# A two-layer convolution and feed-forward kernel: the inverse transform of layer–block pairs three to five by float32 products

## The chip, the cores and the metric

The kernel runs on one core of one Trainium2 chip. The engines that matter here are TensorE (PE, with its weight loads as PEld), VectorE (DVE), ScalarE (ACT), GpSimd (POOL) and SyncE (SP), which issues most DMAs. The metric is the device time of one execution in microseconds (us): 1112.5 us before, the median of three runs between 1112.49 and 1115.72 us.

## The reference, cut to what matters

Two layers, each of them a long convolution followed by a gated feed-forward block, on 2048 rows of 512 channels:

```
def _A_ref(u, ...):                      # K: a kernel of 2048 taps per channel
    Kf = rfft(pad(K)); Uf = rfft(pad(u))
    y = irfft(Uf * Kf)[:L]               # a causal convolution along the rows
    return y + u * Dskip
def _B_ref(x, w_gate, w_up, w_down):
    return (silu(x @ w_gate) * (x @ w_up)) @ w_down

x = x + _A_ref(_layernorm(x), ...)
x = x + _B_ref(_layernorm(x), ...)
x = x + _A_ref(_layernorm(x), ...)
x = x + _B_ref(_layernorm(x), ...)
```

## The kernel before

**Blocks and pairs.** The 2048 rows are cut into four blocks of 512. A pair is (layer, block), and the eight pairs run in the order of the table `SEQ`: (0,0), (0,1), (0,2), (1,0), (0,3), (1,1), (1,2), (1,3). Below they are called the first to the eighth pair. Each pair has a convolution (`ssm`, two calls of `ssm_half`, one for each half of the channels) and a feed-forward part (`ffn`, two halves of 256 rows). The first 300 us or so generate the convolution's taps and their spectra, split the feed-forward weights into two half-precision parts, and run the first pairs' convolutions; from there on the loop over pairs runs.

**The convolution.** `forward` transforms a normalised block into four spectra per half. `ssm_half` takes four steps (`s`), one for each spectrum. In each it multiplies the spectra of this block and of earlier ones with the spectra of the taps (L810) and adds them up (L813): block b takes b+1 products. Then L818 and L819 combine the real and imaginary products, and L765, L766, L831 to L843 form the four vectors `v` that are to be transformed back (`r` = 0 to 3). All of this is DVE work on float32 tiles, and a vector `v` has 2 x 256 columns. The spectra of earlier blocks and of the taps come by DMA from SP (L806 into `w`, L808 into `uu`, three buffers each).

**The inverse transform** (`inverse`, L770 to L783) multiplies each `v` with constant matrices on PE and collects two results in one PSUM tile `pi`; `result` (L785 to L791) adds that tile to the block `xt`. There are two forms. Where the pair's place in `SEQ` is below `INV`, PE multiplies the float32 `v` with the float32 constants `ei`: two products of 256 columns. Otherwise (`half`) ACT writes the upper half-precision part of the scaled `v` (L774), DVE writes the rest of it (a call of `stt` at L775, recorded under the helper's line L230, into the tile `yl`), and PE adds up six half-precision products of 256 columns:

```
terms = [(eih[:, r, i, le], yl[:, ly, i]) for i in range(2) for le, ly in ((0, 0), (0, 1), (1, 0))]
```

`result` then scales the sum back (`stt`, L230 again) where the float32 form adds it as it is (L791). The constants `ei` and `eih` lie in the same place, the first quarter of the tile `mix`; `eih` is loaded over `ei` by SP at L743, when the first pair of the half-precision form begins. So that load waits for the last float32 inverse.

**The feed-forward part.** Each half of `ffn` makes five large tiles `pgu` of 48 products of 128x256 (L930, L931, L933) and one small one in `remainder` (L897 to L899), in a PSUM pool of two buffers that `pgu` and `py` share. Each `pgu` is read out by ACT (L936) and DVE (L937), split by ACT (L938) and DVE (L939), and the last products (L945 to L947) go into `py`, which DVE adds to the block row by row (L950). PE can't begin the tile after the next one before DVE has read this one.

**What sets the order.** From the second pair on, the framework's scheduler decides the order on each engine when the kernel is built; on the chip each engine then goes through its list strictly. The convolution of pair i+1 is written ahead of the feed-forward part of pair i, and the read-outs of the feed-forward part and the inverse products have a raised priority (`BOOST`). Where its plan shows DVE free, the scheduler fills it with convolution work of later pairs, as far as buffers and data allow. The convolution of the eighth pair needs the feed-forward result of the fifth, (0,3).

Of the kernel before, what the change touches and what calls it, by code (L numbers as in the profile page):

```python
# [37 lines left out]
TB = 256  # L38
BOOST = 1 << 20
HALF = 2  # L40
INV = 2
LOW = [a for a in range(1, 33) if a % 2] + [8, 16, 24, 32]
SEQ = ((0, 0), (0, 1), (0, 2), (1, 0), (0, 3), (1, 1), (1, 2), (1, 3))

# [31 lines left out]
def kernel(ctx, tc, x, a_re, a_im, b_re, b_im, c_re, c_im, log_dt, d_skip,  # L76
# [663 lines left out]
    def ssm(layer, b):  # L740

        if (layer, b) == SEQ[INV]:
            nc.sync.dma_start(eih, c_eih)  # L743
# [3 lines left out]
    def ssm_half(layer, b, h):  # L747
        first = layer == 0 and b == 0
        half = SEQ.index((layer, b)) >= INV
        hs = slice(h * HD, (h + 1) * HD)  # L750
# [551 lines left out]
```

## Time and profile before

| | |
|---|---|
| median of three runs | 1112.5 us |
| the profiled execution: its own time / its span | 1118.76 us / 1117.0 us |
| granted TensorE clock over the span | 0.982 |
| instructions | 22795 |
| PE busy / DVE busy / ACT busy, share of the span | 93% / 87% / 49% |
| POOL busy, share of the span | 9% |
| HBM traffic over the span | 118 GB/s |
| chain that ended last: DVE / PE / issue / DMA | 43% / 32% / 11% / 7% |

The page's busy shares are means over unlike stages: DVE makes the taps at first, DVE and PE share the middle, and the last 117 us are the feed-forward part of the last pair, in which DVE has little to do. Matmuls are pipelined, so a PE row's duration (272 ns for a product of 128x256 in half precision) is longer than the distance from one start to the next; what such a product costs is read from the starts. The same holds for DVE to a smaller extent. An idle stretch of an engine is put down to the instruction that ended it.

### The profile page before, as it was taken

What the parts mean: (1) busy time and instruction counts of PE and PEld (TensorE: products, weight loads), DVE (VectorE), ACT (ScalarE), POOL (GpSimd) and SP (SyncE); (2) the same over time, 40 slices, a digit from 0 to 9 for tenths busy, and PEclk for the clock granted to TensorE, in tenths of its full rate; (3) what the DMA queues carried; (4) which work ended last, traced back from release to release, by engine and by line L of the source; (5) the groups of instructions that cost most, each with busy time, mean ns of one, the idle gap of its engine ahead of it and who ended that gap; (6) DMA issues with size and microseconds to landing.
All of it is one profiled execution on the core that took longest, in us unless ns stands there. A gap on an engine that the chain in (4) does not pass through costs nothing.

```text
span 1117.0 us, 22795 instructions
## 1 busy us (share of the span) xinstructions
PE 1034.6 (93%) x9302; PEld 812.1 (73%) x9302; DVE 969.8 (87%) x1405; ACT 548.9 (49%) x1093; POOL 105.1 (9%) x163
## 2 busy tenths in 40 slices
PE   2989999998788999899999999989999999999998
PEld 1868888887676768686858677767768686786774
DVE  8999999999999998999999989999994899972221
ACT  6989999942483245464553154524315532143210
POOL 0112222220000010110000011100000000000000
PEclk9989999998999999999999999999999999999999
DMA  5367777767765455422453562354343244302000
GB/s 207 123 174 174 170 169 178 186 182 269 234 214 96 147 158 188 152 76 54 146 141 100 144 210 86 109 167 112 132 138 109 67 138 147 123 20 56 2 25 20
DMA packets 125003, 149.23 MB, mean 134 GB/s; under 512 B 50897, under 2 KB 75985, under 8 KB 124130
## 3 DMA queue, kind: packets, MB, share of 16 engines
q1 hardware_dynamic: 112994, 122.27, 36.1%
q0 software_dynamic: 11904, 25.50, 9.8%
q8 instruction: 73, 1.20, 0.5%
q14 instruction: 32, 0.26, 0.1%
HBM read 97.66 MB, written 33.82 MB: 118 GB/s over the span
## 4 chain that ended last, share of the span: by engine, by line
DVE 43%; PE 32%; issue 11%; DMA 7%; ACT 4%; POOL 2%; SPq 1%; DVEq 0%; POOLq 0%; ACTq 0%
PE pgu L930 5%; PE pgu L933 4%; PE pgu L931 4%; PE pw L542 4%; DVE t L810 4%; DVE yk L813 3%; DVE yk L810 3%; DMA mix<-nn 3%; DVE g L483 3%; PE py L945 3%; PE py L946 2%; PE py L947 2%; DMA n<-xdr 2%; DVE sg L937 2%; DVE g L497 2%
## 5 line engine op out<-in xcount | busy, mean ns | idle before, releaser
L930 PE MATMUL pgu<-mix,wsl 128*128 128x256 f16 x1280 | 300.4, 274 | 11.9 <-DVE sg L937 5.3
L931 PE MATMUL pgu<-mix,wsl 128*128 128x256 f16 x1280 | 300.2, 274 | 0.0
L933 PE MATMUL pgu<-mix,wsl 128*128 128x256 f16 x1280 | 196.2, 274 | 0.0
L945 PE MATMUL py<-wsl,hh 128*128 128x512 f16 (+1 forms) x352 | 136.0, 386 | 17.8 <-DVE xg L950 15.0
L931 PEld LDWEIGHTS <-wsl 128*128 128x128 f16 x1280 | 125.7, 98 | 31.1 <-issue 14.3
L930 PEld LDWEIGHTS <-wsl 128*128 128x128 f16 x1280 | 125.7, 98 | 18.5 <-issue 1.2
L947 PE MATMUL py<-wsl,hl 128*128 128x512 f16 (+1 forms) x352 | 135.7, 385 | 1.9 <-DVE hl L939 1.8
L933 PEld LDWEIGHTS <-wsl 128*128 128x128 f16 x1280 | 125.8, 98 | 15.5
L946 PE MATMUL py<-wsl,hh 128*128 128x512 f16 x320 | 123.8, 387 | 0.0
L936 ACT ACTIVATE sg<-pgu,sc 128x512 f32<-128x512 f32 x80 | 54.5, 681 | 137.0 <-PE pgu L933 136.9
L813 DVE TENSOR_TENSOR yk<-yk,t 128x1024 f32<-128x1024 f32 x96 | 116.7, 1215 | 0.4
L810 DVE TENSOR_TENSOR t<-uu,w 128x1024 f32<-128x1024 f32 x96 | 116.6, 1215 | 0.1
L937 DVE SCALAR_TENSOR_TENSOR sg<-pgu,sc,sg 128x512 f32<-128x512 f32 x80 | 59.5, 744 | 54.6 <-ACT sg L936 54.5
L938 ACT ACTIVATE hh<-sg 128x512 f16<-128x512 f32 x80 | 50.2, 627 | 86.9 <-DVE sg L937 86.9
L542 PE MATMUL pw<-kt,ek 128*128 128x256 f32 (+1 forms) x384 | 90.8, 373 | 0.0
L542 PEld LDWEIGHTS pw<-kt,ek 128*128 128x128 f32 x384 | 72.3, 193 | 8.5
L946 PEld LDWEIGHTS <-hh 128*128 128x128 f16 (+1 forms) x352 | 34.9, 99 | 56.8 <-issue 21.7
L507 PE MATMUL pk<-re,g 128*32 128x64 f32 x1024 | 65.1, 317 | 2.7 <-DMA g<-g 1.6
L939 DVE TENSOR_TENSOR hl<-sg,hh 128x512 f16<-128x512 f32 x80 | 54.7, 684 | 14.4 <-ACT hh L938 14.4
L947 PEld LDWEIGHTS <-hl 128*128 128x128 f16 (+1 forms) x352 | 34.9, 99 | 43.4 <-issue 3.0
L508 PE MATMUL pk<-im,g 128*32 128x64 f32 x1024 | 63.2, 301 | 0.0
L945 PEld LDWEIGHTS <-hh 128*128 128x128 f16 (+1 forms) x352 | 34.9, 99 | 35.6 <-issue 2.9
(265 smaller groups left out, 2007.1 us busy)
## 6 DMA issues: line engine op xcount, KB each, us to landing
uu<-udr SPq DMA_DIRECT2D x96, 256.0 KB, 3.0
w<-wdr SPq DMA_DIRECT2D x96, 256.0 KB, 2.7
g<-g POOLq DMA_DIRECT2D x6, 1024.0 KB, 9.1
udr<-fu POOLq DMA_DIRECT2D x22, 256.0 KB, 2.9
udr<-u SPq DMA_DIRECT2D x16, 256.0 KB, 3.4
n<-xdr SPq DMA_DIRECT2D x4, 1024.0 KB, 7.1
kdr<-ks SPq DMA_DIRECT2D x6, 512.0 KB, 3.1
kt<-kdr SPq DMA_DIRECT2D x24, 128.0 KB, 3.0
```

The costliest lines, as they stand in the source:

```text
L507: PE.matmul(o, lhsT=g[:, 0, :, d], rhs=re[:, 0:64, d], start=True, stop=False, tile_position=(0, 32 * grp))
L508: PE.matmul(o, lhsT=g[:, 1, :, d], rhs=im[:, 0:64, d], start=False, stop=True, tile_position=(0, 32 * grp))
L542: PE.matmul(pw[:, i], lhsT=e, rhs=kt[:, :, c + 4 * k0:4 * k1:4, :].rearrange("p g k d -> p k g d"), start=c == 0, stop=c == 3)
L810: V.tensor_tensor(t, uu.unsqueeze(2).to_broadcast([P, NQ, 2, 2, DC]), w.unsqueeze(3).to_broadcast([P, NQ, 2, 2, DC]), OP.mult)
L813: V.tensor_tensor(yk, yk, t, OP.add)
L930: PE.matmul(o, lhsT=wgu(wi, k, 0)[:, fs], rhs=nh[:, k], start=k == 0, stop=False)
L931: PE.matmul(o, lhsT=wgu(wi, k, 1)[:, fs], rhs=nh[:, k], start=False, stop=False)
L933: PE.matmul(o, lhsT=wgu(wi, k, 0)[:, fs], rhs=nlo[:, k], start=False, stop=k == 3)
L937: V.scalar_tensor_tensor(sg, pgu[:, 1], sc6[:, 4:5], sg, OP.mult, OP.mult)
L945: PE.matmul(py[:, r], lhsT=hh[:n, f, rc], rhs=wd(f, 0)[:n], start=f == 0, stop=False)
L946: PE.matmul(py[:, r], lhsT=hh[:n, f, rc], rhs=wd(f, 1)[:n], start=False, stop=False)
L947: PE.matmul(py[:, r], lhsT=hl[:n, f, rc], rhs=wd(f, 0)[:n], start=False, stop=f == FT - 1)
```

## The change

One constant. The first five pairs take the float32 form of the inverse transform instead of the first two.

```
@@ -38,7 +38,7 @@
 TB = 256
 BOOST = 1 << 20
 HALF = 2
-INV = 2
+INV = 5
 LOW = [a for a in range(1, 33) if a % 2] + [8, 16, 24, 32]
 SEQ = ((0, 0), (0, 1), (0, 2), (1, 0), (0, 3), (1, 1), (1, 2), (1, 3))
```

Each of the three pairs has eight inverses (two halves, four `r`). Counted in the order of all engines, 24 of the 48 ACT parts (L774) and 24 of the 48 DVE parts (L230 into `yl`) are gone, 144 of the 288 half-precision products too; 48 float32 products stand in their place, and 12 of the 24 scaled results become plain additions (L791). The load of `eih` moves from the third pair to the sixth. Since the scheduler plans anew, much else moves.

DVE at the third pair's first inverses (a piece of the difference; `bb`, `mix` and `xf` hold vectors, results and the block, `yl` the half-precision parts, `sg` and `hl` the feed-forward read-out):

```order
 L835 TENSOR_TENSOR mix<-bb 128x256
 L839 TENSOR_TENSOR bb<-bb,mix 128x512
-L230 SCALAR_TENSOR_TENSOR yl_4065<-bb,sy,yl_4065 128x512
 L810 TENSOR_TENSOR t<-uu,w 128x1024
 L842 TENSOR_TENSOR bb<-bb 128x256
 L843 TENSOR_TENSOR bb<-bb 128x256
-L230 SCALAR_TENSOR_TENSOR yl_4065<-mix,sy,yl_4065 128x512
-L937 SCALAR_TENSOR_TENSOR sg_3034<-pgu,sc_92,sg_3034 128x512
-L813 TENSOR_TENSOR yk<-yk,t 128x1024
-L230 SCALAR_TENSOR_TENSOR yl_4065<-bb,sy,yl_4065 128x512
```

The half-precision parts leave DVE's list here, and the read-out L937 and the sums L813 are set anew around them.

DVE between two read-outs of the fourth pair's feed-forward part (the first two L937 of its second half), before:

```order
L937 SCALAR_TENSOR_TENSOR sg_3034<-pgu,sc_92,sg_3034 128x512
L810 TENSOR_TENSOR yk<-fu,w0r 128x1024
L939 TENSOR_TENSOR hl<-sg_3034,hh 128x512
L883 TENSOR_TENSOR nn_3010<-nn_3010 128x512
L813 TENSOR_TENSOR yk<-yk,t 128x1024
L283 TENSOR_TENSOR fu<-fbt,fu 128x2x4x64
L818 TENSOR_TENSOR mix<-yk 128x256
L819 TENSOR_TENSOR mix<-yk 128x256
L810 TENSOR_TENSOR t<-uu,w 128x1024
L937 SCALAR_TENSOR_TENSOR sg_3034<-pgu,sc_92,sg_3034 128x512
```

And the same place of the changed kernel:

```order
L937 SCALAR_TENSOR_TENSOR sg_3034<-pgu,sc_92,sg_3034 128x512
L810 TENSOR_TENSOR yk<-fu,w0r 128x1024
L939 TENSOR_TENSOR hl<-sg_3034,hh 128x512
L813 TENSOR_TENSOR yk<-yk,t 128x1024
L283 TENSOR_TENSOR fu<-fu 128x2x4x64
L818 TENSOR_TENSOR bb<-yk 128x256
L819 TENSOR_TENSOR bb<-yk 128x256
L810 TENSOR_TENSOR t<-uu,w 128x1024
L290 TENSOR_TENSOR fu<-fbt 128x4x64 x4
L765 TENSOR_TENSOR bb<-bb 128x512
L810 TENSOR_TENSOR yk<-fbt,w0r 128x1024
L937 SCALAR_TENSOR_TENSOR sg_3034<-pgu,sc_92,sg_3034 128x512
```

One product L810 more, the four L290 of a forward transform and an L765 have come between the two read-outs, and the L883 of a normalisation has left.

SP at the load of `eih`, where it stands in the changed kernel:

```order
L236 DMA xf<-xdr 128x4x512
L236 DMA n<-xdr 128x4x512
L806 DMA w<-wdr 128x512
L808 DMA uu<-udr_115 128x512
L743 DMA mix<-in_c_eih_dram 128x2048
L806 DMA w<-wdr 128x512
L808 DMA uu<-udr_115 128x512
```

Before, L743 stood between two such `w` and `uu` loads at the third pair; now it stands between those of the sixth, after the loads of that pair's block (`xf`, `n`).

More of the change, by code (lines that the diff above doesn't have):

```diff
@@ L40 @@
 HALF = 2
-INV = 2
+INV = 5
 LOW = [a for a in range(1, 33) if a % 2] + [8, 16, 24, 32]
```

## The prediction

> **What bounds the kernel now.** I read the busy time of each engine by stretches first, cut at read-outs of the feed-forward part. The columns are the stretch, its length, the busy time of PE, PEld, DVE, ACT and POOL with the number of instructions, the granted clock, the DMA share and GB/s.
>
> ```profile
> core 0: us, PE busy (x) PEld busy (x) DVE busy (x) ACT busy (x) POOL busy (x), PEclk, DMA share, GB/s
> 424.50:766.40 341.90, 321.91 (x2666) 246.88 (x2665) 327.14 (x491) 155.75 (x306) 29.85 (x37) 0.99 0.41 128
> 766.40:841.20 74.80, 71.39 (x565) 50.23 (x563) 71.87 (x102) 22.06 (x39) 3.36 (x7) 0.98 0.46 137
> 841.20:1000.00 158.80, 156.62 (x1326) 121.63 (x1324) 135.96 (x189) 59.93 (x114) 5.85 (x7) 1.00 0.34 102
> ```
>
> From 424.5 to 841.2 us DVE is busy all but 14.8 and 2.9 us, and PE is idle for 20.0 and 3.4 us. After 841.2 us PE has next to no idle time and DVE has 22.8 us of it. So DVE sets the pace up to 841, PE from there to the end. The three pairs that change have their convolutions in the first of these stretches. Who waits there is in the list of waits, PE's two longest entries (424.5 to 841.2 us) and all of DVE's (424.5 to 766.4 us); the columns are the total, the number and the longest.
>
> ```profile
> PE py L945 <- DVE xg L950: 7.1, 3, 3.8
> PE pgu L930 <- DVE sg L937: 4.0, 3, 2.5
> ```
>
> ```profile
> DVE yl L230 <- ACT yl L774: 3.9, 3, 1.8
> DVE rs L226 <- POOL rs L225: 3.3, 5, 0.9
> DVE sg L937 <- ACT sg L936: 3.0, 1, 3.0
> DVE hl L939 <- ACT hh L938: 1.5, 1, 1.5
> DVE sg L908 <- ACT sg L907: 1.1, 1, 1.1
> DVE nn L883 <- DMA mix<-nn: 1.1, 1, 1.1
> DVE sg L906 <- ACT sg L905: 0.5, 1, 0.5
> ```
>
> PE waits for read-outs that stand late in DVE's list, behind convolution work. DVE's own waits are 14.4 us, 3.9 of them for the ACT part of the half-precision form.
>
> So the end is set by one sum: when DVE gets through a late read-out, plus the PE work that is left after that tile. I take two read-outs as marks. Mark A is the last L950 of the first pair; up to it both kernels have the same list. Mark B is the third L937 in the fifth pair's feed-forward part. A third one, C, is the first L937 of that part's second half. Their rows in the timeline of DVE (start, duration), each with the row that follows it:
>
> ```profile
> 423.73 0.74 DVE L950 SCALAR_TENSOR_TENSOR xg<-py,sc,xg 128x512 f32<-128x512 f32 x1
> 424.39 1.21 DVE L813 TENSOR_TENSOR yk<-yk,t 128x1024 f32<-128x1024 f32 x1
> ...
> 765.63 0.74 DVE L937 SCALAR_TENSOR_TENSOR sg<-pgu,sc,sg 128x512 f32<-128x512 f32 x1
> 766.29 1.21 DVE L813 TENSOR_TENSOR yk<-yk,t 128x1024 f32<-128x1024 f32 x1
> ...
> 801.50 0.74 DVE L937 SCALAR_TENSOR_TENSOR sg<-pgu,sc,sg 128x512 f32<-128x512 f32 x1
> 802.16 0.41 DVE L842 TENSOR_TENSOR mix<-mix 128x256 f32<-128x256 f32 x1
> ```
>
> By the start of the next row, A ends at 424.4, B at 766.3 and C at 802.2 us.
>
> **The prices.** A row costs DVE the distance to the next start, not its duration:
>
> ```profile
> 722.59 0.74 DVE L230 SCALAR_TENSOR_TENSOR yl<-bb,sy,yl 128x512 f16<-128x512 f32 x1
> 723.25 0.41 DVE L818 TENSOR_TENSOR mix<-yk 128x256 f32<-128x256 f32 x1
> 723.58 0.41 DVE L819 TENSOR_TENSOR mix<-yk 128x256 f32<-128x256 f32 x1
> 723.92 1.21 DVE L810 TENSOR_TENSOR t<-uu,w 128x1024 f32<-128x1024 f32 x1
> 725.05 0.68 DVE L230 SCALAR_TENSOR_TENSOR fu<-pf,fbt 128x512 f32<-128x512 f32 x1
> 725.65 0.68 DVE L765 TENSOR_TENSOR mix<-bb,mix 128x512 f32<-128x512 f32 x1
> ```
>
> That is 0.66 us for `yl` (a scaled result and L937 alike), 0.335 for 256 columns, 1.135 for 1024 and 0.60 for a plain 512. On PE the same reading gives
>
> ```profile
> 719.43 0.71 PE L782 MATMUL pi<-yl,mix 128*128 128x256 f16 x5
> 719.98 0.27 PE L275 MATMUL pf<-z,eh 128*128 128x256 f16 x1
> ...
> 383.62 1.03 PE L782 MATMUL pi<-mix 128*128 128x256 f32 x4
> 384.49 0.60 PE L933 MATMUL pgu<-mix,wsl 128*128 128x256 f16 x4
> ...
> 718.57 0.38 PE L945 MATMUL py<-wsl,hh 128*128 128x512 f16 x1
> 718.78 0.38 PE L946 MATMUL py<-wsl,hh 128*128 128x512 f16 x1
> ...
> 723.49 0.21 PE L898 MATMUL pgu<-wsl,mix 128*128 128x96 f16 x1
> 723.53 0.21 PE L899 MATMUL pgu<-wsl,mix 128*128 128x96 f16 x1
> ```
>
> 0.11 us for a half-precision product of 256 columns, 0.216 for one of 512, 0.04 for one of 96, and 0.87 for the four records that two float32 products leave.
>
> **The change part by part.** *PE*: an inverse takes 0.87 instead of 6 x 0.11 = 0.66 us, and 24 of them make +5.0 us. All of it comes before mark B, where PE waits 20 us for DVE, so it is hidden there; with that cover gone it would cost its 5.0. *ACT*: 24 parts fewer. ACT sleeps half of the first stretch, so that alone is worth nothing. *DVE*: 24 x 0.66 for `yl` and 12 x 0.06 for the results make -16.6 us over all. If the list stayed as it is, the read-outs of this stretch would come earlier by that much. It doesn't stay so. Counted in the order of both kernels, from mark A to mark B stand on DVE:
>
> | rows of | before | changed | price, us | difference, us |
> |---|---|---|---|---|
> | 1024 columns | 123 | 138 | 1.135 | +17.0 |
> | plain, 512 | 133 | 154 | 0.60 | +12.6 |
> | `yl`, scaled results, read-outs, 512 | 93 | 58 | 0.66 | -23.1 |
> | 256 columns | 118 | 132 | 0.335 | +4.7 |
> | small ones (4.4 us) | the same | the same | | 0 |
> | sum, us | 325.1 | 336.2 | | +11.1 |
>
> The scheduler fills the room with later pairs' products: 15 more rows of L810, L813 and their like stand ahead of the same read-out. So mark B is due later, not earlier. Only at the end of the fifth pair's part is DVE's list shorter, by 13.3 us in the same prices; by then the convolutions it may do are done, since the eighth pair's needs the fifth's result, and PE is the bound.
>
> After the tile of mark B, PE has in both kernels 1920 products of 256 columns, 528 of 512 and 336 of 96 columns left. By the prices (as means of many starts 0.1095, 0.2165 and 0.043) that is 339 us. Before, it took 1117.0 - 766.3 = 350.7 us. Of the 11.6 us above the sum, 3.8 fell between B and C, where DVE still held PE: 35.9 us for 32.1 us of PE's products, with 34.1 us of DVE's rows. In the changed order DVE's rows from B to C take 33.5 us and PE's 34.8, so I let these 3.8 go: 346.9 us from B to the end.
>
> DVE's idle time between A and B is what no row gives. Before, it was 341.9 - 325.1 = 16.8 us, the 14.4 of the list and gaps too small for it. The wait for the ACT part of `yl` goes, 3.9 us, and I keep the rest: 12.9 us. The lower end is 4 us, if only the waits for POOL's L225 (3.3 us) and little else stay. The upper end is the 16.8, and waits on PE that the new form brings: an addition L791 must wait for the float32 products, and a vector may be overwritten only when PE has read it. In the two pairs that have the form now, the list of those who waited for the inverse products says
>
> ```profile
>   DVE bb L834: 0.8, 1
>   DVE xg L791: 0.6, 1
> ```
>
> which is 0.7 us per pair, 2.1 for three, or at most 4.2 if each of the three pairs paid all of it.
>
> *SP*: the load of `eih` waits for the last float32 inverse, and the loads queued behind it wait too.
>
> ```profile
> SPq L743 <- PE pi L782: 4.6, 1, 4.6
> ```
>
> These 4.6 us cost DVE nothing then, because the next loads were not due. In the new order the load behind L743 needs a buffer that DVE frees only after it has added the last result of the fifth pair (L791), which itself waits for that same inverse. So SP would stand still there anyway: zero, and 4.6 us at most.
>
> **The sum.** 424.4 + 336.2 + 12.9 + 346.9 = 1120.4 us of span against 1117.0: **3.4 us slower**. The profiled execution took 1118.76 us where the median of the runs is 1112.5, so I carry the difference over: 1115.9, say 1116 us. The ends: 4 us of idle time gives 1111.5, that is -5.5; 16.8 + 4.2 gives 1128.5, that is +11.5. A measurement of this kernel can tell about 0.3%, 3.3 us, from no change, and the forecast stands right at that line.
>
> **A rule on PE's clock** bears on the size of the waits. The longest wait in the first entry of the list above stopped PE for 3.78 us, and afterwards its products were slow:
>
> ```profile
> 732.91 0.59 PE L945 MATMUL py<-wsl,hh 128*128 128x512 f16 x1 [3.78 <-DVE xg L950]
> 733.29 0.63 PE L946 MATMUL py<-wsl,hh 128*128 128x512 f16 x1
> ...
> 736.22 0.38 PE L947 MATMUL py<-wsl,hl 128*128 128x512 f16 x1
> 736.43 0.38 PE L945 MATMUL py<-wsl,hh 128*128 128x512 f16 x1
> ```
>
> Eight products took 3.3 us instead of 1.7. The new order has more room for such waits: between the first two L937 of the fourth pair's second half stand 9.0 us of DVE rows (6.5 before) for a tile of 48 x 0.11 = 5.3 us. While DVE is the bound, 1.6 us of slow products vanish in PE's next wait; at the last wait before the pace changes hands they would be paid, and for two such waits the time would be 1119.2 us. The Trainium skill, page "TensorE: Matmul & The Clock Gate", section "Part 1: The HAM clock gate", says that the array falls to half its clock after an idle window of about 3.4 us and needs about 3.4 us of work to get it back. The 3.78 us and the 3.3 us agree with it. By that rule a change that lengthens PE's waits costs more than the waits; by the rows it costs that only where PE doesn't wait again, so the forecast leaves it out.
>
> **The rivals.** (1) *The filler closes DVE's gaps: faster.* DVE's 12.9 us of idle time between A and B are places where its list ran ahead of PE, ACT or POOL. With 15 more large rows ahead of the read-outs, it would seldom run ahead, and idle time falls to 4 us: -5.5 us, 1107.0 us. It turns faster than before as soon as more than 3.4 of the 12.9 go. For it: the 3.0 and 1.5 us waits were for ACT, which had to wait for an input load, and the like may fall elsewhere. Against it: the waits for POOL's L225 and for ACT come from the normalisation of later blocks, which both kernels do in the same steps. (2) *DVE's saving counts in full.* PE's waits shrink with DVE's work, and 13.3 us less at the end of the fifth pair's part plus 3.9 less of waiting, minus 5.0 on PE, gives -12, 1100 us. Against it: the sum at mark B, which no shorter list behind B can mend. (3) *New waits on PE and SP.* L791, overwritten vectors and `eih` add 4.2 and 4.6 us: +12.2, 1124.7 us. (4) *The clock*, as above, 1119.2 us. That the change doesn't do what it says is excluded by the order: 24 fewer `yl` rows on DVE and on ACT.
>
> **How the numbers follow.** The forecast has a chance of 0.50; its own range of -1 to +8 us lies with 0.22 within 0.3% and with 0.28 above it. Rival 1 has 0.22 (0.12 faster, 0.10 same), rival 2 0.04 (0.02 and 0.02, as part of it may come), rival 3 0.16 (all slower) and rival 4 0.08 (0.04 same, 0.04 slower). Together: faster 0.14, same 0.38, slower 0.48. The predicted time is 1116.0 us. The range from 1107 to 1124 us reaches from rival 1's time to just short of both costs of rival 3 together; the forecast's own is 1111.5 to 1120.5 us.
>
> **What would show it.** DVE busy without a break from 424 us to the fifth pair's read-outs, mark B near 773.5 us, PE's waits for L937 and L950 together longer than the 11.1 us above, most of them in the fourth pair's second half and the fifth pair's first; then DVE idle while the fifth pair's part ends, earlier than 841 us. Mark B at 766 or before would prove the idle time wrong; a new entry of DVE waiting for `pi`, or SP waiting at L743 with `w` or `uu` late, would prove rival 3. The forecast fails altogether if PE's waits shrink although the read-outs stand later in DVE's list.

## The result: slower by 1%, beyond the range

| | before | changed |
|---|---|---|
| time, median (lowest to highest), us | 1113.78 (1112.49 to 1115.72) | 1124.8 (1121.89 to 1129.45) |
| ratio to before, 95% interval | | 1.0101 [1.0062, 1.0141] |
| profiled execution: time / span, us | 1118.76 / 1117.0 | 1124.15 / 1122.4 |
| granted clock of that execution | 0.982 | 0.984 |
| span from mark A to B / from B to the end, us | 341.9 / 350.6 | 348.7 / 348.8 |

The predicted time was 1116 us in a range from 1107 to 1124. The direction had the largest chance, the size was missed: +11 us in place of +3.4. The page of the changed kernel begins like this (busy time, share of the span, instructions):

```profile
span 1122.4 us, 22651 instructions
## 1 busy us (share of the span) xinstructions
PE 1036.6 (92%) x9254; PEld 815.5 (73%) x9254; DVE 954.4 (85%) x1381; ACT 532.4 (47%) x1069; POOL 100.8 (9%) x163
```

DVE lost some 15 us of work and PE gained 2 in the records, and yet the span is longer. The three marks in the timeline of DVE of the changed kernel, each with the row behind it (`...` stands for rows left out):

```profile
424.11 0.74 DVE L950 SCALAR_TENSOR_TENSOR xg<-py,sc,xg 128x512 f32<-128x512 f32 x1
424.77 1.21 DVE L813 TENSOR_TENSOR yk<-yk,t 128x1024 f32<-128x1024 f32 x1
...
772.86 0.74 DVE L937 SCALAR_TENSOR_TENSOR sg<-pgu,sc,sg 128x512 f32<-128x512 f32 x1
773.52 0.74 DVE L230 SCALAR_TENSOR_TENSOR yl<-bb,sy,yl 128x512 f16<-128x512 f32 x1
...
808.42 0.74 DVE L937 SCALAR_TENSOR_TENSOR sg<-pgu,sc,sg 128x512 f32<-128x512 f32 x1
809.08 0.68 DVE L765 TENSOR_TENSOR mix<-bb,mix 128x512 f32<-128x512 f32 x1
```

Mark B, predicted for 773.5 us, ends at 773.5. Mark C ends at 809.1, 35.6 us behind it. The stretches from A to B and from B to the end, first of the changed kernel, then of a second profile of the program before (run e1 below), in the columns of the prediction:

```profile
424.90:773.60 348.70, 325.01 (x2630) 249.14 (x2629) 338.35 (x506) 142.61 (x286) 28.77 (x41) 1.00 0.44 138
773.60:1122.40 348.80, 336.01 (x2740) 249.78 (x2737) 209.12 (x294) 105.89 (x196) 8.12 (x13) 0.99 0.25 73
sum 697.50, PE 661.03 PEld 498.92 DVE 547.47 ACT 248.50 POOL 36.88; mean PE 330.51 PEld 249.46 DVE 273.74 ACT 124.25 POOL 18.44
```

```profile
424.70:763.60 338.90, 320.16 (x2679) 246.87 (x2678) 327.06 (x491) 156.09 (x306) 30.23 (x37) 0.99 0.42 129
763.60:1112.80 349.20, 335.83 (x2739) 249.70 (x2736) 235.55 (x333) 108.57 (x199) 10.64 (x17) 0.99 0.28 84
sum 688.10, PE 655.99 PEld 496.56 DVE 562.61 ACT 264.66 POOL 40.87; mean PE 328.00 PEld 248.28 DVE 281.31 ACT 132.33 POOL 20.44
```

Between these two profiles the loss lies between A and B: 348.7 against 338.9 us. There DVE has 15 more instructions and 11.3 us more busy time, and PE is idle for 23.7 us in place of 18.7, though it has more to do. From B to the end the two differ by 0.4 us. Over both stretches the changed kernel is 9.4 us longer: 5.0 us more of PE's busy time and 4.4 us more of its idle time.

### The profile page after: what moved, and what is told of

Its sections match the earlier page's. It is cut to its first block, busy times and chain, and to the rows that moved or that the text cites. A ratio compares the mean times of both kernels' runs of the same rounds, so it can differ in the third digit from the quotient of the medians.

```text
span 1122.4 us, 22651 instructions
## 1 busy us (share of the span) xinstructions
PE 1036.6 (92%) x9254; PEld 815.5 (73%) x9254; DVE 954.4 (85%) x1381; ACT 532.4 (47%) x1069; POOL 100.8 (9%) x163
## 3 DMA queue, kind: packets, MB, share of 16 engines
q1 hardware_dynamic: 112994, 122.27, 35.6%
## 4 chain that ended last, share of the span: by engine, by line
PE 34%; DVE 25%; issue 6%; DMA 6%; ACT 2%; SPq 1%; POOL 0%; DVEq 0%; ACTq 0%; POOLq 0%
PE pgu L930 6%; PE pgu L933 6%; PE pgu L931 6%; PE py L945 4%; PE py L946 3%; PE py L947 3%; DVE yk L813 3%; DVE t L810 3%; DVE yk L810 3%; DMA mix<-nn 3%; PE pi L782 2%; DVE sg L937 2%; DMA n<-xdr 1%; PE pw L542 1%; DVE hl L939 1%
## 5 line engine op out<-in xcount | busy, mean ns | idle before, releaser
L930 PEld LDWEIGHTS <-wsl 128*128 128x128 f16 x1280 | 125.5, 98 | 17.5
L936 ACT ACTIVATE sg<-pgu,sc 128x512 f32<-128x512 f32 x80 | 54.5, 682 | 174.3 <-PE pgu L933 170.9
L813 DVE TENSOR_TENSOR yk<-yk,t 128x1024 f32<-128x1024 f32 x96 | 116.9, 1218 | 0.4
L810 DVE TENSOR_TENSOR t<-uu,w 128x1024 f32<-128x1024 f32 x96 | 116.9, 1218 | 0.2
L937 DVE SCALAR_TENSOR_TENSOR sg<-pgu,sc,sg 128x512 f32<-128x512 f32 x80 | 59.7, 746 | 64.5 <-ACT sg L936 61.2
L542 PE MATMUL pw<-kt,ek 128*128 128x256 f32 (+1 forms) x384 | 93.9, 383 | 0.0
L542 PEld LDWEIGHTS pw<-kt,ek 128*128 128x128 f32 x384 | 75.3, 200 | 8.8
L939 DVE TENSOR_TENSOR hl<-sg,hh 128x512 f16<-128x512 f32 x80 | 54.9, 686 | 17.5 <-ACT hh L938 17.5
```

What stands on the lines that cost most here:

```text
L542: PE.matmul(pw[:, i], lhsT=e, rhs=kt[:, :, c + 4 * k0:4 * k1:4, :].rearrange("p g k d -> p k g d"), start=c == 0, stop=c == 3)
L810: V.tensor_tensor(t, uu.unsqueeze(2).to_broadcast([P, NQ, 2, 2, DC]), w.unsqueeze(3).to_broadcast([P, NQ, 2, 2, DC]), OP.mult)
L813: V.tensor_tensor(yk, yk, t, OP.add)
L930: PE.matmul(o, lhsT=wgu(wi, k, 0)[:, fs], rhs=nh[:, k], start=k == 0, stop=False)
L937: V.scalar_tensor_tensor(sg, pgu[:, 1], sc6[:, 4:5], sg, OP.mult, OP.mult)
L939: V.tensor_tensor(hl[:, f0:f0 + 2], sg, hh[:, f0:f0 + 2], OP.subtract)
```

## The experiments

Two theories stood at the start. The **list theory** is the prediction's: the time is what DVE's list ahead of a late read-out takes, plus PE's products behind it. For each kernel I formed the largest such sum from its order and the prediction's prices, and expected times to differ as the sums do. The **products theory** is the rival: the float32 products, at 0.87 us in place of 0.66 for one inverse, cost their own time on PE, and DVE's list matters little.

**e1, e2, e3, e4: another number of pairs.** Only the value of `INV` differs (2 is the program before, 5 the changed one; they were run again to have a second profile of each):

```
INV = 2      (e1; 5 in e2, 6 in e3, 3 in e4)
```

> The kernel before, unchanged (two pairs in float32). It gives a second profiled execution to set the first one's 1118.76 us right. If that first one was a late execution, this span comes out near 1113 us (1.8 us less than the time), and mark B (the third L937 in the fifth pair's feed-forward part) lies at 766 us or a few us earlier. If profiling as such adds about 5 us, the span is 1117 again. Ratio 1.00.

> The changed kernel, unchanged (five pairs in float32). List theory (DVE's order puts more rows ahead of the read-outs): mark B again at 773.5 +- 1 us; ratio 1.010, or nearer 1.005 if the four runs so far were late ones. Clock theory (float32 products lower the granted clock): its granted clock lies below that of the kernel before in every run.

> Six pairs in float32. Sum of DVE's rows from mark A to the latest read-out and of PE's products after it: 670.5 us here, 675.4 with five pairs, 666.2 before. List theory: about 5 us faster than with five pairs, although PE has 1.7 us more to do; ratio to before 1.003 to 1.006. PE theory (each pair in float32 costs 1.7 us at the end, lists apart): 1.7 us slower than with five pairs. Nothing of the computation is left out.

> Three pairs in float32. The same sum is 663.9 us here (666.2 before). List theory: 2 to 4 us faster than before, ratio 0.997. PE theory: 1.7 us slower, ratio 1.0015. A theory in which every pair costs a third of what the change cost (3.7 us): ratio 1.003.

Measured, as ratios to before: two pairs 0.9995 [0.9981, 1.0009], three 1.0009 [0.999, 1.0028], five 1.0088 [1.0066, 1.011], six 1.0035 [1.0015, 1.0055]. The step from five to six fits the list theory: PE has 1.7 us more to do, and the kernel is 0.5% faster, with 331.4 us of DVE rows up to mark B in place of 336.2. The step from two to three does not: the largest sum falls by 2.3 us (666.2 to 663.9) and the time doesn't fall. The first profile of before also turns out to have been a late execution: the same program spans 1112.8 us in e1, with 13.9 us of DVE's idle time from A to B (339.0 by the rows' own times, less 325.1) where the first had 16.8.

**e5 and e6: one half of the change alone.** In e5, pairs 3 to 5 take the float32 products, and `yl` is still written by ACT and DVE; the results are still added by `stt`, and the load of `eih` moves as in the change. In e6 they keep the half-precision products and DVE's subtraction for the low part is left out; the products that read it read the high part, so the result lacks the low part there. Pieces of the two edits (`...` stands for code left out; `PROD` is 5, and `low` is true from the sixth pair on):

```
 e5   -                if half:
      +                if half and SEQ.index((layer, b)) >= PROD:
                           terms = [(eih[:, r, i, le], yl[:, ly, i]) ...
 e6   -                stt(yl[:, 1], v, sy[:, 0:1], yl[:, 0], OP.subtract)
      +                if low:
      +                    stt(yl[:, 1], v, sy[:, 0:1], yl[:, 0], OP.subtract)
```

> Pairs 3 to 5 use the float32 products, as in the change, but ScalarE still writes the half-precision part (L774) and VectorE still subtracts for the low part (L775) there; nothing reads them. So TensorE has the change's products and VectorE the work of before. Nothing of the result is left out. The sum here is VectorE's rows from mark A to the read-out at which (those rows + TensorE's products after it) is largest, plus those products; it is 666.2 us for two pairs (before), 675.4 for the change, 676.2 here, and the row count at mark B is 335.0 us (325.1 before, 336.2 for the change). List theory (the order of VectorE's rows ahead of the read-outs sets the time): +10 us over before, ratio about 1.009, mark B near 773. Products theory (the longer products cost their own time on TensorE and VectorE's saving counts for nothing): +5 us, ratio 1.0045, mark B near 768. If VectorE's saved 16.5 us had counted in the change, this kernel would be well slower than the change, at +15 us or more.

> The other half alone: pairs 3 to 5 keep the six half-precision products and ScalarE's part, and only VectorE's subtraction for the low part (L775) is gone; the products read the high part in its place, so the low half-precision part of v is left out of the result there. TensorE has the work of before, VectorE 15.8 us less than before. Sum 665.6 us against 666.2 before. List theory: no change, -0.6 us, ratio 0.9995, mark B near 764. If VectorE's saving counted in full: -12 us, ratio 0.989. Products theory: no change or a few us faster.

e5 took 1128.73 us, ratio 1.0139 [1.0118, 1.016], and e6 1115.72 us, ratio 1.0029 [1.0014, 1.0045]. The stretches from A to B of e5 and then of e6:

```profile
426.40:774.00 347.60, 322.99 (x2611) 247.03 (x2610) 335.93 (x503) 156.25 (x307) 27.40 (x38) 1.00 0.42 132
```

```profile
426.50:766.90 340.40, 321.19 (x2662) 245.86 (x2660) 327.28 (x487) 156.72 (x307) 29.82 (x39) 0.98 0.43 135
```

The added DVE time ahead of mark B comes with the products: 335.9 us of DVE's busy time there in e5, 327.3 in e6, 327.1 in e1. The filling itself comes with either half. Of the large rows of 1024 columns, 123 stand between A and B before, 129 in e5, 133 in e6 and 138 with the change; but in e6 they only replace the 24 rows that are gone. By itself the shortened work of DVE gained nothing. It is not worthless next to the products: with them, and without it, the kernel is at 1.0139, with both at 1.0088 to 1.0101. So of the 16.6 us that DVE saves, some 4 to 6 us come back as time. The sizes miss both theories: for e5 the list had +10 us and the products +5 (measured +15), and for e6 the list had nothing (+3).

**e7 and e8: the change, with the products less urgent.** The priority of the products in pairs 3 to 5 is taken back to 0 (e7, shown here) or put below everything (e8: `-BOOST` in place of the last 0):

```
-            with tc.high_priority(offset=0 if first else BOOST):
+            with tc.high_priority(offset=0 if first else (BOOST if half or SEQ.index((layer, b)) < 2 else 0)):
```

> The change with one more edit: the products of pairs 3 to 5 are issued to the scheduler without the raised priority (offset 0 in place of BOOST at L776). The same instructions run on every engine as in the change; only their order differs. VectorE's rows from mark A to mark B are then 317.3 us (336.2 in the change, 325.1 before), and the sum is 661.7 us (675.4 in the change, 666.2 before), its latest read-out now early, in the second pair's part. List theory: 13 us faster than the change and 4 us faster than before, ratio about 0.996. Products theory (+5 us of TensorE's own, and the rest from waits around the longer products): as the change, ratio 1.005 to 1.01. In between, about 1.000, if the products now come so late that a result is waited for by the next part's feed-forward products.

> As the run without raised priority, but with a lowered one (-BOOST) for the products of pairs 3 to 5, so that everything else that is ready goes first. Sum 658.6 us, which is nearly TensorE's own 657.8 us after mark A. List theory taken alone: 7.6 us faster than before, ratio 0.993. Against it: v's buffers are held and the results come late, so the next part may wait for its own x; then it is slower than the run without raised priority, at 1.000 or above, with TensorE's idle time at the start of a pair's feed-forward part waiting for VectorE's normalisation.

e7: 1120.74 us, 1.0072 [1.0053, 1.009]. e8: 1173.2 us, 1.0551 [1.0521, 1.0582], as its expectation feared for late results. Of PE's two longest entries from 400 us on, the first is for the load of `mix`, the next block's normalised input:

```profile
PE pgu L897 <- DMA mix<-nn: 21.5, 4, 9.6
PE py L945 <- DVE xg L950: 13.4, 6, 2.9
```

e7 is a clear miss of the list theory. DVE's rows to mark B fell by 19 us, but the way from A to B only from 348.7 to 343.7 us:

```profile
425.90:769.60 343.70, 326.19 (x2613) 248.78 (x2611) 320.94 (x479) 141.64 (x283) 28.61 (x38) 0.98 0.43 132
```

DVE now waits there for 26.4 us (343.7 - 317.3), where the runs with the raised priority had 12.5 to 16.8. So with the list made short, DVE's list no longer sets the time to B. What does is not shown: PE is idle there for 17.5 us too (343.7 - 326.2). I took up a third theory, **two bounds**: DVE's list and PE's products are nearly level in the kernel before, and the larger one counts.

**e9 and e10: the kernel before with a shorter list, and with a shorter list and less work on PE.** In e9 no inverse product has a raised priority. In e10 those of pairs 3 to 5 have none (a second edit, of the same line as in e9), and only the two products of the high parts are left there; the low parts are still written, so DVE's work is that of before and the result lacks them. `HIGH` is 5.

```
 e9   -            with tc.high_priority(offset=0 if first else BOOST):
      +            with tc.high_priority(offset=0 if first else 0):
 e10  +                if half and SEQ.index((layer, b)) < HIGH:
      +                    terms = [(eih[:, r, i, 0], yl[:, 0, i]) for i in range(2)]
```

> The kernel before (two pairs by float32 products) with offset 0 in place of BOOST at L776 for all pairs: the same instructions as before on every engine, another order. VectorE's list gives a sum of 662.2 us (666.2 before), TensorE's products after mark A stay at 652.8 us. Two-bounds theory (time after mark A is the larger of the list's sum + about 22 us and TensorE's products + about 35.5 us, which in the kernel before are level at 688): the list falls to 684, TensorE's bound stays at 688.3, so no change, ratio 0.998 to 1.001; and the run of five pairs without raised priority, which has this order's freedom too, is slower than this one by TensorE's 5 us. List theory taken alone: 4 us faster, ratio 0.9964. Products cost nothing of their own: this run and that of five pairs without raised priority are equal.

> The kernel before, with only the products of the high parts (2 of 6 per step) in pairs 3 to 5 and offset 0 at L776 there; the products with a low part are left out of the result in those pairs, while the low parts are still written. VectorE's work is that of before, TensorE's products after mark A are 642.3 us (652.8 before), the list's sum 648.9 us (666.2 before). Two-bounds theory: the list gives 671, TensorE 677.8, so about 10 us faster than before, ratio 0.9906, TensorE's idle time after mark A about as before (25 to 28 us). List theory alone: 17 us faster, ratio 0.984. If VectorE's work set the time, which is unchanged: no change, 1.000.

e9: 1106.82 us, 0.9946 [0.9926, 0.9967], faster than both kernels. e10: 1094.83 us, 0.9835 [0.9812, 0.9859]. Here the list theory is right (-4 and -17 us expected, -6 and -18 measured), and the two bounds, with constants fitted to the runs so far, are wrong on both times (no change and -10 us expected): PE's idle time is not a constant, it fell here with the list. After mark A, PE is idle for 27.5 us in e9 (680.80 - 653.28) and for 32.1 in e1:

```profile
426.70:756.80 330.10, 312.84 (x2620) 240.65 (x2618) 317.23 (x477) 148.98 (x292) 25.36 (x36) 0.99 0.43 130
756.80:1107.50 350.70, 340.43 (x2799) 254.99 (x2796) 245.01 (x346) 114.51 (x213) 12.41 (x18) 1.00 0.29 86
sum 680.80, PE 653.28 PEld 495.64 DVE 562.24 ACT 263.50 POOL 37.77; mean PE 326.64 PEld 247.82 DVE 281.12 ACT 131.75 POOL 18.89
```

**e11 and e12: five and four pairs by float32 products, in the order rule of e9.** Only `INV` differs from e9 (5 and 4).

> The change (five pairs by float32 products) with offset 0 at L776 for all pairs, as in the run of two pairs without raised priority, so that the two differ in the products and VectorE's rows alone. VectorE's list: sum 661.7 us (662.2 with two pairs), largest early, in the second pair's part; at mark B the rows are 310.2 us against 315.4. TensorE's products after mark A: 657.8 us against 652.8. List theory: as the run of two pairs, ratio 0.994. Own cost of the products: 5 us above that run, ratio 0.999, as TensorE has no idle time that would take them up. As the run that lowered the priority in pairs 3 to 5 alone: 1.007, which would say that some 9 us come from waits that the list's sum does not show.

> Four pairs by float32 products, offset 0 at L776 for all. List's sum 660.0 us, TensorE's products after mark A 656.1 us. List theory: 2 us faster than two pairs without raised priority, ratio 0.9925. Own cost of the products: 3.3 us slower than two pairs, ratio 0.9975, between two and five pairs.

e11: 1117.53 us, 1.0039 [1.0024, 1.0055]. e12: 1113.89 us, 1.0009 [0.9993, 1.0026]. Both have shorter lists than e9 and both are slower: 0.63% for two pairs more, 0.93% for three. The list theory is out for this rule. The change costs about the same under either rule: 0.93% here, 0.88 to 1.01% with the raised priority. That is some 10 us, twice the 5.0 us of the products' own time. In e11, from A:

```profile
420.80:761.90 341.10, 324.49 (x2611) 247.99 (x2609) 313.85 (x469) 141.55 (x283) 29.28 (x37) 0.98 0.42 131
761.90:1110.60 348.70, 336.74 (x2759) 251.29 (x2757) 233.85 (x331) 107.96 (x198) 10.37 (x17) 1.00 0.29 84
sum 689.80, PE 661.23 PEld 499.28 DVE 547.70 ACT 249.51 POOL 39.65; mean PE 330.61 PEld 249.64 DVE 273.85 ACT 124.75 POOL 19.83
```

PE is busy 7.95 us longer than in e9 and idle 1.05 us longer; DVE waits 30.9 us on the way to mark B (341.1 - 310.2).

**The runs side by side**, after mark A, in us. DVE's rows up to A are the same in all of them, and yet A comes between 420.7 and 426.6 us, so the table counts from there. e8 is left out, as it waits for other things. The second column is PE's products by the prices; the third, PE's busy time above these; the fourth, its idle time; the last two, DVE's rows from A to B by the prices, and the rest of that way.

| run | products | above | PE idle | DVE rows A to B | DVE idle A to B |
|---|---|---|---|---|---|
| before, first profile | 652.8 | 6.6 | 33.1 | 325.1 | 16.8 |
| e1, before again | 652.8 | 3.2 | 32.1 | 325.1 | 13.9 |
| the change | 657.8 | 3.2 | 36.5 | 336.2 | 12.5 |
| e2, the change again | 657.8 | 4.8 | 35.8 | 336.2 | 14.7 |
| e3, six pairs | 659.5 | 1.2 | 30.6 | 331.4 | 14.3 |
| e4, three pairs | 654.5 | 5.7 | 30.9 | 324.8 | 15.3 |
| e5, products only | 657.8 | 3.4 | 39.7 | 335.0 | 12.7 |
| e6, DVE only | 652.8 | 4.6 | 30.4 | 324.9 | 15.5 |
| e7, change, pairs 3 to 5 not raised | 657.8 | 4.8 | 31.3 | 317.3 | 26.4 |
| e9, before, none raised | 652.8 | 0.5 | 27.5 | 315.4 | 14.7 |
| e10, high parts only | 642.3 | 0.3 | 25.7 | 302.0 | 11.0 |
| e11, five pairs, none raised | 657.8 | 3.4 | 28.6 | 310.2 | 30.9 |
| e12, four pairs, none raised | 656.1 | 2.5 | 29.9 | 312.7 | 26.8 |

Two groups can be seen in the last column. With 11 to 17 us I read DVE's list as what sets when mark B comes. With 26 to 31 us it isn't: these three have a short list and the longer products. The second column is counted, not measured; but with 1.6 us for each half-speed stretch (last section) PE's busy time is this count to within 1.1 us in every run, so the products' 5.0 us is work that PE does in full under either rule. What the other half of the change's 10 us is, no run here separates.

## Why the prediction was wrong

The step that failed is the sum's two credits, 3.9 and 3.8 us, together with the offset: the credits were taken from terms of one late profile, were larger than what the runs show, and the same profile's lateness was then taken off once more.

**Mark B: the rows right, the idle time by luck.** 773.5 us was predicted from 336.2 us of DVE rows and 12.9 us of idle time; it came at 773.5, with 12.5 of idle time. (With the prices as printed the two sums of rows are 324.7 and 335.9; the difference stays.) The scheduler's larger stock of later pairs' work ahead of the read-outs is the mechanism, and e5 shows that the products bring 10 us of it. The idle time came right because its base was too high and the credit taken from it too large, by about as much (next paragraph). PE's waits grew in the fourth pair's second half, as predicted: those for L937 and L950 are 5.6 us there in both profiles of the change, 2.3 and 2.7 before. In the fifth's first half they shrank, from 4.3 and 3.1 to 2.3, and in the second pair's second half they grew from 0.7 to 3.8, which the prediction had not named. PE's waits of the changed kernel, A to B, the longest entries:

```profile
PE py L945 <- DVE xg L950: 4.7, 2, 2.5
PE pgu L930 <- DVE xg L950: 3.9, 1, 3.9
PE py L947 <- DVE hl L939: 3.3, 3, 1.5
PE pgu L897 <- DVE sg L937: 3.1, 2, 1.7
PE py L945 <- DVE sg L937: 2.7, 1, 2.7
PE pgu L930 <- DVE sg L937: 1.7, 2, 1.4
PE py L945 <- DVE xf L950: 1.5, 1, 1.5
```

Those for L937 and L950 are 17.6 us together, against 12.6 in e1 and 13.8 in the first profile. The 11.1 us that the prediction set as the bar were two entries of that list only, over a longer stretch, so the bar was too low; the waits grew all the same.

**The credit of 3.9 us for the wait on ACT's `yl`: mis-sized, and this is the step that failed first.** The prediction said: "The wait for the ACT part of `yl` goes, 3.9 us, and I keep the rest: 12.9 us." That wait did go. It heads the first list here, of DVE's longest waits in e1 from A to B, and is not among those of the changed kernel:

```profile
DVE yl L230 <- ACT yl L774: 3.3, 2, 1.8
DVE rs L226 <- POOL rs L225: 3.3, 5, 0.9
DVE sg L937 <- ACT sg L936: 1.8, 1, 1.8
DVE hl L939 <- ACT hh L938: 1.5, 1, 1.5
```

```profile
DVE sg L937 <- DMA uu<-udr: 3.3, 1, 3.3
DVE hl L939 <- ACT hh L938: 3.0, 2, 2.2
DVE rs L226 <- POOL rs L225: 1.7, 3, 0.9
DVE fbt L230 <- ACT fu L276: 1.4, 1, 1.4
```

Others took its place. Idle time from A to B is 13.9 us with the waits for `yl` (e1) and 12.5 and 14.7 without them (the change twice): a saving of -0.8 to 1.4 us, not 3.9. The 16.8 us from which 3.9 was taken belonged to a late execution.

**The credit of 3.8 us behind mark B: mis-sized.** "So I let these 3.8 go: 346.9 us from B to the end." The two profiles of the change have 348.8 and 347.4, those of before 350.6 and 349.2. The means differ by 1.8 us. From B to C most of the credit did come: 35.6 and 35.5 us for 34.8 us of products, where before took 35.9 and 34.8 for 32.1. Behind C the products left are fewer by 2.7 us, but the stretch is shorter by only 2.0 us in the means.

**The offset: in part taken off twice.** The span forecast, 1120.4 us, lies between the two profiles of the changed kernel, 1122.4 and 1119.8. What missed is the sentence "so I carry the difference over", which took 6.26 us off for the first profile's distance to the median. But a part of that distance was the first profile's own: 1117.0 against 1112.8 us of span in e1. It had 2.9 us more of idle time before B and 1.4 us more from B to the end, and these are the two terms from which the credits had been taken already. (It was not the wait for `yl` that made it late; that is 3.9 us there and 3.3 in e1.) With the usual 1.75 us between span and time (1124.15 - 1122.4), the sum would have read 1122.2 us, inside the range and close to the 1123.0 and 1124.8 measured. Put as differences from e1 to the change: +11.1 of rows, -1.4 of idle time and -0.4 behind B make +9.3, and the profiles show +9.4, where the sum had +11.1, -3.9 and -3.8.

**PE's 5.0 us: hidden as the sum had it, but with less cover than it seemed.** The prediction had it where "PE waits 20 us for DVE, so it is hidden there". While DVE's list sets mark B, the 5.0 us is no further term: mark B came on time without it. But it does not shrink PE's waits, which went from 18.7 to 23.7 us. And where the list was shortened (e7, e11, e12) the cover seems gone. e11 against e9 is 10 us by the ratios: 5.0 are products, 2.9 busy time above them in the profiles, 1.1 idle time. The 2.9 us are for the most part half-speed stretches (last section): two in e11's profile, one of them of double length, and one in e9's. The profiled execution of e11 is the shortest of its twelve (1112.43 us against a median of 1117.53), so what the 10 us are made of in the others stays open.

**The rivals.** Rival 1 (filler closes DVE's gaps, 4 us of idle time) is excluded by 12.5 and 14.7. Rival 2 (DVE's saving in full, -12 us) is excluded by the result, and by e6, which has DVE's shorter rows alone and is not faster. Rival 3 gave the nearest time, 1124.7, for the wrong reason: in the changed kernel's profile DVE never waits for `pi` between A and B (0.9 us in its second one), and SP's wait at L743 is 3.2 us with nothing late behind it. The 3.3 us that its list puts on a load of `uu` is a wait for ACT: the L936 that this L937 needs starts at 440.56 us, just before DVE goes on at 441.27, behind a normalisation that had waited 3.75 us for a load of `n`. The second profile has the same wait, 3.28 us, under ACT's name, and the first profile of before had one of 3.0. Rival 4, the clock, is taken up in the last section; the change has two slow stretches after mark A, as e1 has, so the difference between these two owes it nothing.

## What to carry to other kernels

Price a re-ordered kernel from the counted rows against a typical execution, and not against one profile: an idle time read from a single late profile is credited once as a saving and a second time when the sum is brought to the median. A second profile of the same program (4.2 us apart here) is worth more than a finer count. When a product is made longer and the vector work shorter, look at what the scheduler does with the list first, and don't count the product as covered: here the change cost twice the products' own time under both order rules, and taking the raised priority away from the products of the kernel before was the edit that paid (0.9946).

## What the runs showed of the hardware that was not expected

PE's half-speed stretches don't begin where a wait ends, and don't need the longest ones. In the changed kernel, after a wait of 3.93 us, the timeline of PE shows full speed at first, one product each 0.11 us. The four products from 707.15 us on take 0.90 us in place of 0.60, and from there it is one each 0.21 us until 710.8:

```profile
706.28 0.27 PE L930 MATMUL pgu<-mix,wsl 128*128 128x256 f16 x1 [3.93 <-DVE xg L950]
706.39 0.27 PE L931 MATMUL pgu<-mix,wsl 128*128 128x256 f16 x1
...
707.15 0.90 PE L933 MATMUL pgu<-mix,wsl 128*128 128x256 f16 x4
707.84 0.42 PE L930 MATMUL pgu<-mix,wsl 128*128 128x256 f16 x1
...
710.78 0.27 PE L930 MATMUL pgu<-mix,wsl 128*128 128x256 f16 x1
```

In e1 a wait of 2.16 us brought such a stretch 1.2 us after its end, and one of 3.15 us at 730 us brought none:

```profile
689.83 0.27 PE L930 MATMUL pgu<-mix,wsl 128*128 128x256 f16 x1 [2.16 <-DVE xg L950]
...
691.23 0.42 PE L930 MATMUL pgu<-mix,wsl 128*128 128x256 f16 x1
691.44 0.42 PE L931 MATMUL pgu<-mix,wsl 128*128 128x256 f16 x1
...
730.17 0.38 PE L945 MATMUL py<-wsl,hh 128*128 128x512 f16 x1 [3.15 <-DVE xg L950]
730.38 0.38 PE L946 MATMUL py<-wsl,hh 128*128 128x512 f16 x1
```

The granted clock explains both. In each profile the half-speed stretches after mark A start at whole multiples of 3.41 us from each other and, but for one that runs into the end, last 3.41 us or a multiple of it. Cut along this grid, e1 looks like this around the two waits (stretch, length, PE's busy time, granted clock, DMA share, GB/s):

```profile
687.62:691.03 3.41, 1.25 (x13) 1.00 0.24 69
691.03:694.44 3.41, 3.41 (x19) 0.50 0.57 158
725.17:728.58 3.41, 1.85 (x40) 1.00 0.01 5
728.58:731.99 3.41, 1.82 (x9) 1.00 0.20 77
```

The wait of 2.16 us fell whole into one stretch of the grid, and the next one ran at half clock. The wait of 3.15 us was split, 1.56 and 1.59 us, and none did. The 14 profiles have 2770 such stretches at full clock after 424 us. All in which PE was idle, by its rows, for more than 2.06 us were followed by one at half clock, and none with less than 1.87 us was; between the two figures both occur, and 37 were followed in all. So what counts here is how a wait falls on the grid, and the grid differs from one execution to the next: those of the two profiles of before lie 0.75 us apart.

The Trainium skill, page "TensorE: Matmul & The Clock Gate", section "Part 1: The HAM clock gate", says that the window of about 3.4 us over which activity is judged is free-running and doesn't reset when a kernel starts. The grid agrees with that; that some 2 us of idle time in one window are enough is not what its "idle window" suggests. Counted from the starts, each stretch costs some 1.6 us. The first profile of before has four after mark A and e1 two, so in PE's busy time some 3.2 of the 4.2 us between two profiles of one program are these; whether they made the first one late is not shown, as DVE sets the pace where three of the four lie. e9 has one and e10 none. They make up nearly all of the column "above" in the table.
